# Sixteen small block moves inside SBUF, or two stores to DRAM and eight gathers: the rows of the global tokens

## The chip, the cores and the metric

The program runs on one core of a Trainium2 chip. The metric is the device time of one execution in microseconds (us), lower is better; the time of the kernel before is the median of three runs. A profiled execution comes with a trace, and times inside it are counted from the start of its span.

## The reference

Banded attention with a few global tokens, then two multilayer perceptrons, all in float32:

```python
# attention: 4 batches, 8 heads, 512 local rows (a band of +-32 keys and the 32 global keys),
# 32 global rows that see all 544 keys; head size 64
x = attn_out.transpose(0, 2, 1, 3).reshape(B * S, H * D)      # 2176 rows of 512
h = x @ w_in                                                  # 512 -> 2048
g = np.where(h > 0.0, h, np.exp(np.minimum(h, 0.0)) - 1.0)
x = g @ w_out                                                 # 2048 -> 512
h = x @ w_in2
g = np.where(h >= 1, h, np.where(h <= -1, 0.0, (h + 1) ** 2 / 4.0))
y = g @ w_out2
```

## The kernel before

Precision is kept by splitting each float32 operand into a high and a low part of the type that TensorE multiplies at full rate; a product is three matmuls (low weight by high data, high by low, high by high). The 2176 rows fall into 4 x 512 local rows, handled as wide tiles of 128 x 512, and 4 x 32 = 128 global rows, called group `GR`, handled apart. This change touches only the global rows.

For the local rows one layer is: matmuls up (`up`, lines L283 and L1107; most pairs go through a scheme of seven products instead of eight on pre-added forms of the operands, the tiles `form` in DRAM and `xh`, `xl` in SBUF, loaded at L1070), the activation on ScalarE (L303 to L310) and VectorE (`join`, L315 and L317), a split into `gh` (ScalarE, L332) and `gl` (VectorE, L336), and matmuls down (`dn`, L370). A finished down bank leaves PSUM through ScalarE into `ev` (L349) and from there by DMA into a sum in DRAM: a plain store from the SP queue (L352), or an accumulating DMA from the POOL queue (L354). The last part of a layer is added on VectorE instead (L357, tiles `sum` and `sums`).

The global rows go through the same layers eight times, each time for four blocks of 128 hidden columns; these eight passages are called stages 1 to 8 here. In a stage the operands of the up product stand the other way round (`row_products`, L295): the 128 rows are on the partitions of the result, 4 x 128 hidden columns beside them. The down product (`down_rows`, L383) needs the hidden columns on the partitions, so each 128 x 128 block must be transposed. VectorE transposes 32 x 32 blocks in place (L1201, tile `blocks`), and 16 DMAs from the SP queue put the blocks where they belong (L1207, tile `turned`). Then ScalarE makes the high part and VectorE the low part of `turned`, and TensorE may begin L383.

What sets the order: up to the end of attention instructions stand in the order written. From there (some 200 us into the span until the end) a scheduler places them on each engine's queue by its own estimate of durations; each engine then runs its queue strictly in order, and the SP queue, which issues nearly all DMAs, does too. A DMA from SP also waits for the DMA that stands eight before it on that queue to have landed. Buffers that matter: `u` (6 buffers: `blocks`, `turned` and the partial sums), `gh`/`gl` (6 each), `wraw` (2, packed weights as loaded at L869).

Of the kernel before, what the change touches and what calls it, by code (L numbers as in the profile page):

```python
# [9 lines left out]
F32 = mybir.dt.float32  # L10
BF16 = mybir.dt.bfloat16
F32R = mybir.dt.float32r
U32 = mybir.dt.uint32
U64 = mybir.dt.uint64
AF = mybir.ActivationFunctionType
ALU = mybir.AluOpType
# [5 lines left out]
B, H, SL, SG, D = 4, 8, 512, 32, 64  # L22
# [4 lines left out]
P = 128  # L27
# [51 lines left out]
def band_attention_then_two_mlps(  # L79
# [45 lines left out]
    dram = ctx.enter_context(tc.tile_pool(name="dram", bufs=1, space=bass.MemoryType.DRAM))  # L125
# [29 lines left out]
    eng = pinned  # L155
# [106 lines left out]
    def h_tile(name):  # L262

        i = held[0] // 2 % (H_EARLY + (H_MORE if len(h_p) > 1 else 0))
        held[0] += 1
        return h_p[i >= H_EARLY].tile([P, SL], F32R, tag=name, name=name)
# [159 lines left out]
    def mpool(name, bufs, **kw):  # L426
        return ctx.enter_context(tc.tile_pool(name=name, bufs=bufs, reuse_waits="tile", **kw))
# [4 lines left out]
    with ExitStack() as actx:  # L432
# [371 lines left out]
        for n in range(len(units) + 2):  # L804
# [25 lines left out]
            if n == 1:  # L830
                rows = eye_sb.rearrange("p (c h r) -> p c h r", c=2, h=2)
# [14 lines left out]
        eng = free  # L846
# [4 lines left out]
    u_p = mpool("u", 6, side="right")  # L851
# [332 lines left out]
    def rows(layer, fs, pieces):  # L1184

        def begin():
            need(lambda: all(piece in rows_in for piece in pieces))
            n = len(fs) * P
            u = Up(layer, None, GR, n=n)
            u.row_products(pieces)  # L1190
            u.curve()
            u.join()
            soon.setdefault(now[0] + 1, []).append(lambda: blocks(u))
            item[1] = now[0] + 4
            item[2] = u

        def blocks(u):

            n = len(fs) * P
            t = u_p.tile([P, SL], F32, tag="u", name="blocks")  # L1200
            eng.vector.transpose(t[:, :n], u.g)  # L1201
            u.g = u_p.tile([P, SL], F32, tag="u", name="turned")[:, :n]
            for e in range(4):
                out = u.g[32 * e:32 * e + 32].rearrange("p (f r q) -> p f r q", r=4, q=32)
                for r in range(4):
                    src = t[32 * r:32 * r + 32, :n].rearrange("p (f e q) -> p f e q", e=4, q=32)
                    eng.sync.dma_start(out[:, :, r], src[:, :, e])  # L1207
            u.high()
            u.low()

        item = ["rows", None, None, layer, fs]
        return begin, item
# [51 lines left out]
    def need(done):  # L1264

        tries = 0
        while not done():
            step(line[0])
            tries += 1
            assert tries < 100, "what is needed is not under way"  # L1270
# [53 lines left out]
    for c in range(7):  # L1324
        at = base + 17 * c
# [110 lines left out]
```

## Time and profile before

| what | us |
|---|---|
| median of three runs (lowest to highest) | 825.73 (824.58 to 828.87) |
| the profiled execution's own time | 829.02 |
| its span in the trace | 827.2 |
| TensorE matmul busy in the span | 804.7 |
| VectorE / ScalarE / POOL busy | 678.8 / 544.3 / 86.5 |
| DMA, mean rate over the span | 211 GB/s |

The profiled execution took 3.29 us longer than the median run, and its own time is 1.82 us longer than its span. Busy times of different engines overlap; matmuls are pipelined, so TensorE's row tells when it had work, not how fast the work went.

### The profile page before, as it was taken

The page shows a single profiled execution, that of the slowest core. Times are in us where ns is not written, and L with a number is a line of the kernel's source. Part 1 is how long each engine was busy: PE and PEld are TensorE (multiplying, and loading weights), DVE is VectorE, ACT ScalarE, POOL GpSimd, SP SyncE. Part 2 cuts the span into 40 slices and gives each one's busy share as a digit, 9 for nine tenths or more (in the row PEclk, how much of TensorE's full clock was granted, in tenths as well). Part 3 has the DMA queues.
Part 4 walks back from the last instruction along what each step waited for, and adds up shares of the span by engine and source line. Part 5 has one row for each costly group of instructions (what it writes and reads, how often), then busy time and mean ns, then how long its engine had stood idle before and what let it go on. Part 6 is the DMA issues. An engine that isn't in the chain of part 4 may idle for free.

```text
span 827.2 us, 15959 instructions
## 1 busy us (share of the span) xinstructions
PE 804.7 (97%) x6038; PEld 659.7 (80%) x6038; DVE 678.8 (82%) x1271; ACT 544.3 (66%) x928; POOL 86.5 (10%) x146
## 2 busy tenths in 40 slices
PE   7889899999999999999999999999999999999998
PEld 4667678888887888888888788888888888888876
DVE  4879888997987999966879999999997798745464
ACT  4778875765655667555636687777867786666361
POOL 2222210000011030301100000000110203011000
PEclk9999999999999999999999999999999999999999
DMA  8988845878686498829917948347871996289523
GB/s 268 288 268 252 276 152 186 331 278 311 199 327 103 124 281 279 177 39 225 331 45 254 377 152 314 111 146 260 266 172 33 264 317 108 36 198 289 185 104 115
DMA packets 82109, 174.60 MB, mean 211 GB/s; under 512 B 27376, under 2 KB 27632, under 8 KB 80880
## 3 DMA queue, kind: packets, MB, share of 16 engines
q1 hardware_dynamic: 72528, 156.53, 55.4%
q0 software_dynamic: 9216, 16.78, 13.0%
q8 instruction: 48, 0.79, 0.4%
q10 hardware_dynamic: 288, 0.26, 0.1%
q14 instruction: 29, 0.24, 0.1%
HBM read 112.46 MB, written 58.98 MB: 207 GB/s over the span
## 4 chain that ended last, share of the span: by engine, by line
PE 78%; DMA 8%; ACT 5%; DVE 5%; SPq 3%; issue 2%; ACTq 0%; DVEq 0%
PE dn L370 36%; PE up L1107 25%; PE up L283 4%; PE up L295 2%; SPq L1207 2%; PE dn L383 2%; PE s L147 2%; DMA turned<-blocks 2%; ACT sn L147 1%; DMA wraw<-in_w 1%; PE po L147 1%; DMA form<-xl 1%; PE pt L147 1%; DVE sum L357 1%; PE up L147 1%
## 5 line engine op out<-in xcount | busy, mean ns | idle before, releaser
L370 PE MATMUL dn<-gh,wo 128*128 128x512 f32 x608 | 182.8, 390 | 0.9 <-DVE sums L357 0.9
L863 DVE TENSOR_TENSOR u<-up,u 128x512 f32<-128x512 f32 x182 | 121.7, 683 | 35.7 <-PE up L1107 34.9
L1107 PE MATMUL up<-xh,ws 128*128 128x512 f32 x416 | 140.2, 389 | 0.2 <-DVE u L863 0.2
L370 PEld LDWEIGHTS dn<-gh,wo 128*128 128x128 f32 x608 | 113.8, 188 | 24.7 <-DVE sums L357 1.3
L1107 PE MATMUL up<-xh,wi 128*128 128x512 f32 x376 | 126.1, 389 | 0.0
L354 POOL DMA_DIRECT2D sum<-ev x64 | 58.2, 1188 | 581.8 <-ACT ev L349 553.8
L370 PE MATMUL dn<-gl,wo 128*128 128x512 f32 x304 | 113.4, 389 | 0.0
L332 ACT ACTIVATE gh<-g 128x512 fp32r<-128x512 f32 x123 | 76.7, 628 | 45.6 <-DVE g L315 26.5
L336 DVE TENSOR_TENSOR gl<-g,gh 128x512 fp32r<-128x512 f32 x123 | 83.6, 683 | 11.6 <-ACT gh L332 11.3
L1107 PEld LDWEIGHTS up<-xh,ws 128*128 128x128 f32 x416 | 78.1, 188 | 16.8 <-DVE u L863 0.6
L1107 PEld LDWEIGHTS up<-xh,wi 128*128 128x128 f32 x376 | 70.6, 188 | 14.6
L1107 PE MATMUL up<-xl,ws 128*128 128x512 f32 x208 | 80.9, 389 | 0.0
L1107 PE MATMUL up<-xl,wi 128*128 128x512 f32 x188 | 73.2, 389 | 0.0
L308 ACT ACTIVATE g<-u,half_sb 128x512 f32<-128x512 f32 x56 | 40.4, 722 | 39.9 <-DVE u L863 36.5
L370 PEld LDWEIGHTS dn<-gl,wo 128*128 128x128 f32 x304 | 57.1, 188 | 11.9
L349 ACT ACTIVATE ev<-dn 128x512 f32<-128x512 f32 x96 | 53.0, 598 | 15.1 <-PE dn L370 14.5
L370 PE MATMUL dn<-gh,xl 128*128 128x512 f32 x160 | 62.4, 390 | 0.1
L370 PE MATMUL dn<-gh,xh 128*128 128x512 f32 x160 | 62.3, 389 | 0.0
L370 PE MATMUL dn<-gl,xh 128*128 128x512 f32 x160 | 60.9, 390 | 0.0
L317 DVE TENSOR_TENSOR g<-u,g 128x512 f32<-128x512 f32 x56 | 38.4, 685 | 19.7 <-ACT g L310 19.6
L309 ACT ACTIVATE g<-g,one_sb 128x512 f32<-128x512 f32 x68 | 49.0, 721 | 1.5
L303 ACT ACTIVATE g<-u 128x512 f32<-128x512 f32 x48 | 30.2, 629 | 27.2 <-DVE u L863 23.7
(195 smaller groups left out, 1525.1 us busy)
## 6 DMA issues: line engine op xcount, KB each, us to landing
wraw<-in_w SPq DMA_DIRECT2D x56, 512.0 KB, 7.5
xh<-form SPq DMA_DIRECT2D x42, 512.0 KB, 9.0
xl<-form SPq DMA_DIRECT2D x42, 512.0 KB, 8.0
v_sb<-in_vwin SPq DMA_DIRECT2D x64, 260.0 KB, 4.8
sum<-ev POOLq DMA_DIRECT2D x64, 256.0 KB, 7.9
form<-xh SPq DMA_DIRECT2D x24, 512.0 KB, 4.8
form<-xl SPq DMA_DIRECT2D x24, 512.0 KB, 5.5
sum<-ev SPq DMA_DIRECT2D x32, 256.0 KB, 4.6
```

The source lines that it names most:

```text
L147: return lambda *args, **kw: tc.keep_in_program_order(fn(*args, **kw))
L283: eng.tensor.matmul(self.ps, w, x, start=k == 0, stop=k == 3 * KT - 1)
L308: eng.scalar.activation(self.g, self.ps, AF.Relu, bias=half_sb, scale=-0.5)
L309: eng.scalar.activation(self.g, self.g, AF.Relu, bias=one_sb, scale=-1.0)
L317: eng.vector.tensor_tensor(g, self.ps, g, ALU.max)
L332: eng.scalar.activation(self.gh, self.g, AF.Copy)
L336: eng.vector.tensor_tensor(self.gl, self.g, self.gh.bitcast(F32), ALU.subtract)
L349: eng.scalar.activation(out, ps, AF.Copy)
L354: eng.gpsimd.dma_start(to, out, accum_op=ALU.add)
L370: eng.tensor.matmul(banks[d], w[:, d * P:(d + 1) * P], g, start=first and k == 0, stop=last and k == 2)
L863: return eng.vector.tensor_tensor(out, a, b, op)
L1107: eng.tensor.matmul(ps, w[:, a, at + k * P:at + (k + 1) * P], x[b][:, k * SL:(k + 1) * SL], start=onto is None and k + t == 0, stop=not mo ...
```

## The change

In each of the eight stages the split into high and low parts is made before the blocks are moved, in the order in which VectorE's transpose left them. The high part goes into a second `u` tile (`high`), the low part is left in `blocks`. Each part is stored to DRAM whole (128 x 512, 256 KB, tile `rows`), and four gathers each read it back from DRAM into 32 partitions of `gh` or `gl` at a time, in runs of 32 elements (128 bytes). ScalarE and VectorE no longer touch the moved data; TensorE waits for the gathers themselves.

```diff
             t = u_p.tile([P, SL], F32, tag="u", name="blocks")
-            eng.vector.transpose(t[:, :n], u.g)
-            u.g = u_p.tile([P, SL], F32, tag="u", name="turned")[:, :n]
-            for e in range(4):
-                out = u.g[32 * e:32 * e + 32].rearrange("p (f r q) -> p f r q", r=4, q=32)
-                for r in range(4):
-                    src = t[32 * r:32 * r + 32, :n].rearrange("p (f e q) -> p f e q", e=4, q=32)
-                    eng.sync.dma_start(out[:, :, r], src[:, :, e])
-            u.high()
-            u.low()
+            low = t[:, :n]
+            eng.vector.transpose(low, u.g)
+            high = u_p.tile([P, SL], F32, tag="u", name="high")[:, :n]
+            eng.scalar.activation(high.bitcast(F32R), low, AF.Copy)
+            eng.vector.tensor_tensor(low.bitcast(F32R), low, high, ALU.subtract)
+            u.gh, u.gl = (h_tile(name)[:, :n] for name in ("gh", "gl"))
+            for out, part in ((u.gh, high), (u.gl, low)):
+                kept = dram.tile([P, n], F32, name="rows")
+                eng.sync.dma_start(kept, part)
+                src = kept.rearrange("(r p) (f e q) -> e p f r q", r=4, e=4, q=32)
+                for e in range(4):
+                    at = out[32 * e:32 * e + 32].rearrange("p (f r q) -> p f r q", r=4, q=32)
+                    eng.sync.dma_start(at.bitcast(F32), src[e])
```

The scheduler places the new instructions elsewhere than the old ones, and others around them. On the SP queue, at stage 1 (`sum` are stores of finished banks, `form` the loads of operands for the next local products), a piece of the difference, - is before and + is the change:

```order
-L352 DMA sum_3_110<-ev 128x512
-L1207 DMA turned<-blocks 32x4x32 x14
+L352 DMA sum_3_110<-ev 128x512 x4
+L1209 DMA rows<-high 128x512
+L1070 DMA xl<-form_0_0_115 128x1024
+L1209 DMA rows<-blocks 128x512
 L1070 DMA xh<-form_0_0_115 128x1024
-L1070 DMA xl<-form_0_0_115 128x1024
+L1213 DMA gh<-rows 32x16x32 x4
+L1213 DMA gl<-rows 32x16x32 x4
```

The 16 moves make way for ten DMAs, the stores come behind all four sums, and two loads of forms, which stood behind the moves, now stand between the stores and ahead of the gathers.

On ScalarE at stage 2, before, the high part of the moved rows (`gh<-turned`) stands in the middle of the queue, ahead of two other splits and three evictions of down banks:

```order
L215 ACTIVATE top<-wraw 128x1024
L349 ACTIVATE ev<-dn 128x512
L332 ACTIVATE gh<-turned 128x512
L332 ACTIVATE gh<-g 128x512 x2
L349 ACTIVATE ev<-dn 128x512 x3
L239 ACTIVATE wo<-top 128x1024
```

In the change the high part is made far ahead of that place, beside the split that follows the transpose:

```order
L303 ACTIVATE g<-u 128x512
L1204 ACTIVATE high<-blocks 128x512
L305 ACTIVATE g<-g,one_sb 128x512
L922 ACTIVATE ws<-mixed 128x1024
L332 ACTIVATE gh<-g 128x512
L215 ACTIVATE top<-wraw 128x1024
```

and where it stood, the evictions follow with nothing of the global rows among them:

```order
L239 ACTIVATE wo<-top 128x1024
L332 ACTIVATE gh<-g 128x512
L349 ACTIVATE ev<-dn 128x512
L215 ACTIVATE top<-wraw 128x1024
L349 ACTIVATE ev<-dn 128x512 x2
```

What moved is the instruction that waited for the moves: nothing on ScalarE waits for a DMA of the global rows any more. On VectorE at stage 8 (`sum<-dn` empties the four down banks of local rows), before:

```order
L317 TENSOR_TENSOR g<-u,g 128x512
L336 TENSOR_TENSOR gl<-turned,gh 128x512
L317 TENSOR_TENSOR g<-u,g 128x512
L863 TENSOR_TENSOR u<-up,u 128x512
L336 TENSOR_TENSOR gl<-g,gh 128x512
L357 TENSOR_TENSOR sum<-dn,sum 128x512 x2
```

and with the change:

```order
L317 TENSOR_TENSOR g<-u,g 128x512 x2
L863 TENSOR_TENSOR u<-up,u 128x512
L336 TENSOR_TENSOR gl<-g,gh 128x512
L357 TENSOR_TENSOR sum<-dn,sum 128x512
L336 TENSOR_TENSOR gl<-g,gh 128x512
```

The low part has left this place; it stands right behind the transpose there.

## Rows read from the trace of the kernel before

**Rows 1.** The page: engines' busy time, TensorE's clock by slices, chain that ended last.
```profile
PE 804.7 (97%) x6038; PEld 659.7 (80%) x6038; DVE 678.8 (82%) x1271; ACT 544.3 (66%) x928; POOL 86.5 (10%) x146
...
PEclk9999999999999999999999999999999999999999
...
PE dn L370 36%; PE up L1107 25%; PE up L283 4%; PE up L295 2%; SPq L1207 2%; PE dn L383 2%; PE s L147 2%; DMA turned<-blocks 2%; ACT sn L147 1%; DMA wraw<-in_w 1%; PE po L147 1%; DMA form<-xl 1%; PE pt L147 1%; DVE sum L357 1%; PE up L147 1%
```
**Rows 2.** Stretches of TensorE: from:to, busy us (matmuls), granted clock, DMA share, GB/s.
```profile
240.00:250.00 10.00, 10.00 (x46) 1.00 0.77 209
...
260.00:270.00 10.00, 8.57 (x38) 1.00 0.50 70
...
460.00:470.00 10.00, 9.12 (x41) 1.00 1.03 394
...
790.00:800.00 10.00, 9.18 (x39) 1.00 0.45 157
```
**Rows 3.** The waits of TensorE: line, who released it, us in total, times, longest.
```profile
PE dn L383 <- ACT ev L349: 1.4, 1, 1.4
...
PE dn L370 <- DVE sums L357: 0.9, 1, 0.9
...
PE dn L383 <- DVE sum L357: 0.7, 1, 0.7
```
**Rows 4.** Timeline of stage 2, ScalarE, then TensorE: start, us, what, [idle before <- releaser].
```profile
262.18 0.63 ACT L332 ACTIVATE gh<-turned 128x512 fp32r<-128x512 f32 x1 [5.76 <-DMA turned<-blocks]
...
263.76 1.55 ACT L349 ACTIVATE ev<-dn 128x512 f32<-128x512 f32 x3
...
265.37 0.50 PE L383 MATMUL dn<-xl,gh 128*128 128x512 f32 x1 [1.43 <-ACT ev L349]
```
**Rows 5.** Timeline of stage 8, VectorE, then TensorE.
```profile
789.53 0.69 DVE L336 TENSOR_TENSOR gl<-turned,gh 128x512 fp32r<-128x512 f32 x1 [6.34 <-ACT gh L332]
...
793.74 1.28 DVE L357 TENSOR_TENSOR sum<-dn,sum 128x512 f32<-128x512 f32 x2
...
795.16 0.47 PE L383 MATMUL dn<-xl,gh 128*128 128x512 f32 x1 [0.66 <-DVE sum L357]
```
**Rows 6.** DMAs of three lines: us to issue, and to landing (min/median/max).
```profile
L1207 SPq DMA_DIRECT2D turned<-blocks x128: 585/599/1557, 204.3 to 785.5; - x128
...
DMA to landing us min/median/max: 1.8/2.2/10.8
...
L406 SPq DMA_DIRECT2D outT<-rows_sum x4: 632/638/645, 806.2 to 808.2; - x4
...
DMA to landing us min/median/max: 2.2/2.2/2.2
...
L352 SPq DMA_DIRECT2D sum<-ev x32: 319/328/1128, 151.7 to 574.0; - x32
...
DMA to landing us min/median/max: 2.4/4.6/9.9
```
**Rows 7.** Timeline of the SP queue at stage 1, then two rows of L383.
```profile
206.50 0.54 SPq L352 DMA_DIRECT2D sum<-ev  x1
207.09 9.13 SPq L1207 DMA_DIRECT2D turned<-blocks  x14
216.32 0.53 SPq L1070 DMA_DIRECT2D xh<-form  x1
...
218.72 0.39 PE L383 MATMUL dn<-wl,gh 128*128 128x512 f32 x1
...
223.25 0.39 PE L383 MATMUL dn<-wh,gl 128*128 128x512 f32 x1
```
**Rows 8.** The moves of stages 2 and 7 on the SP queue, and L383 of stage 7.
```profile
244.36 16.19 SPq L1207 DMA_DIRECT2D turned<-blocks  x16
...
683.49 12.00 SPq L1207 DMA_DIRECT2D turned<-blocks  x16
...
706.44 0.62 PE L383 MATMUL dn<-wo,gh 128*128 128x512 f32 x2
```

## The prediction

> **What bounds the kernel now.** I read the page first. TensorE has work for 804.7 of 827.2 us, and its granted clock is full, 9 in all 40 slices [rows 1] and 1.00 in the stretches quoted [rows 2], the level of 2.4 GHz, so the throttle plays no part. What the change can give back is idle time of TensorE, since the number and the size of its matmuls stay the same. The page's chain that ended last seems to offer more: it lists SPq L1207 with 2% and "DMA turned<-blocks" with 2%, together some 33 us. The second view, TensorE by stretches of 10 us, shows how to take that. Between 240 and 250 us, while the moves of stage 2 are under way, TensorE is busy for all 10.00 us [rows 2]. The chain follows a late DMA back through a time in which TensorE had other work. From 130 to 800 us there are 67 stretches, and 64 of them show at least 9.99; the other three miss 1.43, 0.88 and 0.82 us [rows 2], 3.13 us in all. The third view, the waits of TensorE, names them: ScalarE's eviction at L349 held L383 for 1.4 us, VectorE's sums held L370 for 0.9 and L383 for 0.7 [rows 3]. So 3.1 us, 0.4% of the time, is about all that lies there for any change of this part.
>
> The timelines show which of these belong to the global rows. At stage 2 ScalarE sat idle for 5.76 us until the moves had landed, because the high part of `turned` stood next on its queue. The three evictions behind it ran at 263.76, and TensorE, which needed the last bank, began L383 at 265.37 after 1.43 us of idle time [rows 4]. The global rows' data was not what came last; the queue behind it was. At stage 8 it is VectorE: idle for 6.34 us before the low part of `turned`, then the additions that empty the down banks, up to 793.74 + 1.28 = 795.02, and L383 at 795.16 after 0.66 us [rows 5]. The 0.9 us stands between 460 and 470 us, on the tile `sums` at the change of layer, and no L383 lies in that stretch, so I give it no share.
>
> **The change part by part.** *ScalarE and VectorE.* Each stage keeps one activation and one subtraction of the same size, beside the transpose now, with operands that are ready when it ends. Cost: none in busy time. What goes is the wait of these two queues for the DMAs. In front of TensorE that is worth the 1.43 us of stage 2 and the 0.82 us that the stretch at 790 misses, 2.25 together. The waits of the other six stages were hidden, as only these stretches of TensorE have a gap, so nothing comes of them.
>
> *The SP queue.* Sixteen moves of 0.6 us make 9.6 us at the least; stretches of 12.00 us at stage 7 and 16.19 at stage 2 show them with waits between [rows 6, 8]. Two stores now take some 0.33 us each, like L352, 0.66 in all. The first gather must wait until its store has landed: 2.4 us at the least, 4.6 in the median, 9.9 at the most for such a store of 256 KB [rows 6]. No gather of this kind is in the trace. The nearest for its shape is L406, the same 64 KB in the same 128-byte runs, but into DRAM: 0.64 us to issue, 2.2 to land. Eight gathers make 5.1 us of issue. From the first store's issue to the last landing that is 0.33 + 4.6 + 5.1 + 2.2 = 12.2 us in the median, since the second store lands while the first four gathers are issued; 10.0 us with the quickest store, and 0.33 + 9.9 + 5.1 + 10.8 = 26.1 with the slowest store and the slowest landing of a move [rows 6] in place of 2.2. Before it was about as long: 9.6 us of issue, 1.8 to 2.2 of landing and 1.3 for the two splits that followed, 12.7 to 13.1 at best and 19.2 at stage 2 (from 244.36 to 262.18 [rows 4, 8] and the 1.3). What stands behind on SP, loads of weights and forms, is held about as long as before.
>
> *Who waits now.* TensorE's L383 waits for the gathers itself, and behind it stands everything else on TensorE. So each stage needs its room checked. At stage 7 the moves began at 683.49 and L383 ran at 706.44 [rows 8], 22.9 us for a chain of 12.2, or of 16 beside accumulating DMAs as below: hidden. Stages 3 to 6 and 8 have no gap in front of L383 apart from the one explained, and in them the scheduler leaves L383 126 to 133 matmuls behind the last L295, where it stood 126 to 135 behind it. At stage 2 the moves began at 244.36 [rows 8]; the transpose now stands three places later on VectorE, so the store can go at about 246, and L383 stands four places later than before; without the wait it would begin at 265.37 - 1.43 + 0.9, near 264.9. That is 19 us of room, in which the accumulating DMAs from POOL slow everything (that is why the moves took 16.19). A move issued there took up to 10.8 us to land [rows 6]; I take 16 us for the chain, so no wait, with 3 us to spare.
>
> Stage 1 is tightest. In the change the two stores stand behind four sums, the last of them issued at 206.5 [rows 7], so the first goes at about 207. The two loads of forms between the stores and the gathers need buffers that TensorE frees: by their place on its queue (0.227 us a matmul, as the 20 matmuls from 218.72 to 223.25 show [rows 7]) at 206.7 and 208.4, so they hold SP for little. The sums just ahead found the DMAs nearly idle there, so I take 2.6 us for the store, near its least: gathers issued from 209.6 to 214.7, landed at 217 to 218. L383 stands where it began before, at 218.72, and with the low part 0.5 us later; before, the low part was asked for only at 223.25 [rows 7]. So I take no wait, with 1 us to spare; from below it can't gain, as TensorE did not wait there, and above, with the slowest store, the last gather lands at 207 + 0.33 + 9.9 + 5.1 + 2.2 = 224.5, against 219.2: 5.3 us lost.
>
> *The traffic.* Each stage moves 1 MB where 0.25 MB went, 6 MB more on 174.6 MB. The stretches of 10 us show the DMAs anywhere from 0.50 to 1.03 busy [rows 2], so now and then a load comes later; none of TensorE's three waits was for a load [rows 3]. I take nothing for this by itself.
>
> *The new order.* The scheduler lays out TensorE, ScalarE and VectorE anew from stage 1 to stage 3, and in small steps later. Its order of before left 3.13 us of gaps; another one may leave a gap where there was none. Between nothing and the largest single gap, 1.43 us, I take half, 0.7 us.
>
> *The sum* on the profiled execution: 829.02 - 2.25 + 0.7 = 827.5 us. That execution was 3.29 us above the median run, so the same difference, -1.55 us, on the median: 825.73 - 1.55 = **824.2 us**, 0.2% less. A measurement of this kernel can't tell a change of under about 0.5% (4.1 us) from none.
>
> **A rule that speaks against the change.** Before, runs of 128 bytes went from SBUF to SBUF and landed in 1.8 us when nothing else ran [rows 6]; now they are read from DRAM. The Trainium skill (DMA: Bandwidth & Descriptors, section "Why small descriptors are slow (HBM only)") says that small descriptors cost extra where HBM is one end, and that SBUF to SBUF doesn't suffer so. No run so far shows a read of 128 bytes from DRAM; the writes of L406 at 2.2 us speak for a small penalty. By L406 the sum stands as it is; by the rule gathers would land later, which is the third rival.
>
> **The rivals.** *First, the waits only move* (the order of the new layout leaves as much as it gives, or the evictions at stage 2 wait for something else on ScalarE's queue, such as the L215 that now stands among them): 825.7 us. For it: three gaps of about a microsecond in 670 us are what a layout by estimates leaves anyway. Against: the two gaps have one cause each, and it is taken out.
>
> *Second, the chain is right*: the 2% of L1207's issue and the 2% of landings are real, and half of the shares comes back, 16 us, giving 810 us. For it: the page's list. Against: TensorE's busy stretches, which leave no room for over 3.1 us plus the end of the span.
>
> *Third, slower: the gathers are late for L383.* Place: stages 1 and 2, where the room is 1 and 3 us. Price: 5.3 us at stage 1 as above; at stage 2, 246 + 26.1 = 272 against 264.9, 7 us. It decides when a store takes over some 3.6 us to land at stage 1 (2.6 and the 1 us to spare), or store and gathers together take over 19 us at stage 2. Stage 1 alone, at half its price, gives 824.2 + 2.7 = 826.9; both in full, and the 1.4 us of stage 2 not gained, 824.2 + 1.4 + 12.3 = 837.9. For it: at the busiest times stores took 9.9 us and moves 10.8. Against: at 203 to 216 us the queues were light.
>
> **How the numbers follow.** The forecast has 0.60, the first rival 0.20, the second 0.03, the third 0.17, about half of it within 829.9 us (0.5%). The range goes from the lowest run shown less all three gaps, 824.58 - 3.13 = 821.4, down to 821 in round figures, up to 829.5, which takes in the highest run shown (828.87) with no gain and the part of the third rival that costs less than 4 us; left out are the second rival and the dear half of the third, some 0.12 together, and a little of the spread of runs. Faster by over 0.5% needs more than the gaps hold: 0.05, the second rival and chance. Slower by over 0.5%: 0.09. The rest, 0.86, is within 0.5%.
>
> **What would show it.** Right: no wait of ScalarE or VectorE on a DMA of the global rows; full stretches of TensorE at stages 2 and 8; eight stretches on SP of two stores and eight gathers, 9 to 13 us long; gathers landing in some 2 us at quiet times. Wrong: a wait of L383 for "DMA gh<-rows" or "DMA gl<-rows"; gathers that take far over 0.64 us to issue or several us to land with the DMAs idle; new gaps of TensorE elsewhere, at the form loads above all.

## The result, and the profile after

The change is slower: 833.35 us in the median of six runs (830.90 to 834.25) against 824.59 (822.27 to 828.87, six runs), a ratio of 1.0096 with a 95% interval of 1.0070 to 1.0122, about 8 us. The forecast was 824.2, its range 821.0 to 829.5, with 0.09 on slower. The profiled execution of the change took 830.9 us (span 829.1), the least of the six.

In the change L1202 is the transpose, L1204 and L1205 make the high and the low part, L1209 is the stores, L1213 the gathers. First TensorE by stretches, read as in [rows 2]: from:to, length, busy us (matmuls), granted clock, DMA share, GB/s.

```profile
240.00:250.00 10.00, 10.00 (x46) 1.00 1.05 227
260.00:270.00 10.00, 10.00 (x46) 1.00 0.81 199
460.00:470.00 10.00, 7.63 (x34) 1.00 1.03 315
...
610.00:620.00 10.00, 5.88 (x26) 1.00 1.13 207
620.00:630.00 10.00, 9.82 (x36) 0.83 0.10 40
790.00:800.00 10.00, 10.00 (x46) 1.00 0.57 210
```

And the waits of TensorE that answer to [rows 3]:

```profile
PE dn L383 <- DMA gl<-rows: 4.3, 1, 4.3
PE up L1107 <- DVE wi L241: 2.4, 1, 2.4
...
PE dn L370 <- DVE sum L357: 0.4, 1, 0.4
```

The two gaps that the change was to close are closed: the stretches at 260 and 790, which missed 1.43 and 0.82 us, are full. Two others have come. Between 610 and 620 us, in stage 6, TensorE misses 4.12 us, waiting for the low part's gathers, and in the next stretch the granted clock is 0.83, with 36 matmuls where a full stretch has 46. At the change of layer, between 460 and 470 us, it misses 2.37 us where it missed 0.88, and waits for a weight that VectorE unpacks (`wi`, L241).

The second stretch of stage 6 needs a closer look: TensorE's timeline there, then its stretches of 2 us.

```profile
615.26 0.61 PE L383 MATMUL dn<-wo,gh 128*128 128x512 f32 x2
620.18 0.47 PE L383 MATMUL dn<-wo,gl 128*128 128x512 f32 x1 [4.30 <-DMA gl<-rows]
...
621.55 0.63 PE L383 MATMUL dn<-xh,gh 128*128 128x512 f32 x1
621.98 0.63 PE L383 MATMUL dn<-xh,gl 128*128 128x512 f32 x1
```
```profile
620.00:622.00 2.00, 1.82 (x7) 0.80 0.51 201
622.00:624.00 2.00, 2.00 (x6) 0.50 0.00 0
624.00:626.00 2.00, 2.00 (x9) 0.84 0.00 0
626.00:628.00 2.00, 2.00 (x10) 1.00 0.00 0
```

After the idle time the clock was at 0.50, the level of 1.2 GHz, from about 621 to 624 us; matmuls then started 0.43 us apart (621.55 to 621.98) in place of 0.227. The stretch holds 36 matmuls from 620.18 us on, where 43.4 would fit at 0.227 (the 46 of a full stretch count in two that began before it). The 7.4 that are missing cost 1.7 us, as the granted clock of the stretch says too: 10 x (1 - 0.83) = 1.7. So stage 6 lost 4.3 + 1.7 = 6.0 us, the change of layer 2.37 - 0.88 = 1.5, and 2.25 was won: 5.2 us lost in all. The span is only 1.9 us longer than before because its attention part, which the change doesn't touch, was 3.4 us shorter in this execution: the first L295 stands at 185.6 us here and at 189.0 before. 5.2 - 3.4 = 1.8, and the account closes to 0.1 us.

Why the low part was late is read from the SP queue at stage 6, where the transpose ended at 594.7, and from the landings of the two new lines over all stages.

```profile
595.85 0.85 SPq L869 DMA_DIRECT2D wraw<-in_w  x2
596.79 0.42 SPq L1209 DMA_DIRECT2D rows<-high  x1
597.62 0.69 SPq L1209 DMA_DIRECT2D rows<-blocks  x1
606.84 2.61 SPq L1213 DMA_DIRECT2D gh<-rows  x4
609.55 3.27 SPq L1213 DMA_DIRECT2D gl<-rows  x4
```
```profile
L1209 SPq DMA_DIRECT2D rows<-high x8: 319/326/420, 203.1 to 776.1; - x8
L1209 SPq DMA_DIRECT2D rows<-blocks x8: 319/326/745, 204.6 to 776.8; - x8
...
DMA to landing us min/median/max: 2.0/6.1/10.0
```
```profile
L1213 SPq DMA_DIRECT2D gh<-rows x32: 568/628/1616, 206.2 to 784.1; - x32
L1213 SPq DMA_DIRECT2D gl<-rows x32: 563/636/1688, 210.2 to 786.8; - x32
...
DMA to landing us min/median/max: 2.2/2.9/8.8
```

Four accumulating DMAs from POOL and two loads of weights were in flight when the stores went out; the stores took 10 us, and SP stood until 606.84. A second group of four accumulating DMAs began at 608.42, and the gathers of the low part issued among them landed up to 8.8 us later, at 620.04. That is 25.4 us after the transpose, where TensorE began L383 after 20.6 and asked for the low part after 21.2. In the kernel before the sixteen moves of this stage had all landed 13.1 us after the transpose.

### The profile page after: what moved, and what is told of

It reads as the page before. It is cut to its first block, busy times and chain, and to the rows that moved or that the text cites. A ratio compares the mean times of both kernels' runs of the same rounds, so it can differ in the third digit from the quotient of the medians.

```text
span 829.1 us, 15948 instructions
## 1 busy us (share of the span) xinstructions
PE 807.0 (97%) x6038; PEld 661.8 (80%) x6038; DVE 678.7 (82%) x1271; ACT 544.6 (66%) x928; POOL 89.4 (11%) x146
## 5 line engine op out<-in xcount | busy, mean ns | idle before, releaser
L370 PE MATMUL dn<-gh,wo 128*128 128x512 f32 x608 | 183.0, 390 | 0.0
L1107 PE MATMUL up<-xh,ws 128*128 128x512 f32 x416 | 140.3, 389 | 0.0
L370 PEld LDWEIGHTS dn<-gh,wo 128*128 128x128 f32 x608 | 114.1, 188 | 23.5
L1107 PE MATMUL up<-xh,wi 128*128 128x512 f32 x376 | 126.1, 390 | 2.4 <-DVE wi L241 2.4
L354 POOL DMA_DIRECT2D sum<-ev x64 | 60.8, 1225 | 585.5 <-ACT ev L349 555.4
L370 PE MATMUL dn<-gl,wo 128*128 128x512 f32 x304 | 114.0, 390 | 0.0
L1107 PEld LDWEIGHTS up<-xh,ws 128*128 128x128 f32 x416 | 78.1, 188 | 16.2
L336 DVE TENSOR_TENSOR gl<-g,gh 128x512 fp32r<-128x512 f32 x123 | 83.6, 683 | 7.5 <-ACT gh L332 7.4
L1107 PEld LDWEIGHTS up<-xh,wi 128*128 128x128 f32 x376 | 70.6, 188 | 17.4 <-DVE wi L241 2.8
L1107 PE MATMUL up<-xl,ws 128*128 128x512 f32 x208 | 80.9, 389 | 0.0
L1107 PE MATMUL up<-xl,wi 128*128 128x512 f32 x188 | 73.2, 390 | 0.0
L370 PEld LDWEIGHTS dn<-gl,wo 128*128 128x128 f32 x304 | 57.3, 188 | 12.0
L370 PE MATMUL dn<-gh,xl 128*128 128x512 f32 x160 | 62.2, 391 | 0.4 <-DVE sum L357 0.4
L370 PE MATMUL dn<-gh,xh 128*128 128x512 f32 x160 | 62.3, 389 | 0.0
L370 PE MATMUL dn<-gl,xh 128*128 128x512 f32 x160 | 60.2, 389 | 0.0
```

Of the source, the lines that this page charges most:

```text
L336: eng.vector.tensor_tensor(self.gl, self.g, self.gh.bitcast(F32), ALU.subtract)
L354: eng.gpsimd.dma_start(to, out, accum_op=ALU.add)
L370: eng.tensor.matmul(banks[d], w[:, d * P:(d + 1) * P], g, start=first and k == 0, stop=last and k == 2)
L1107: eng.tensor.matmul(ps, w[:, a, at + k * P:at + (k + 1) * P], x[b][:, k * SL:(k + 1) * SL], start=onto is None and k + t == 0, stop=not mo ...
```

## The experiments

Theory A: the trip through DRAM is late in some stage, because its stores and gathers run beside accumulating DMAs. Theory C: the new layout of the engines' instructions loses the time. Further rivals stand where they came up. `before` in a comparison is the kernel before, run on the same chip beside it.

**The change once more.** No edit.

> The change once more, for a second profile, since the profiled execution (830.9 us) was the fastest of its six. In that one TensorE stood still for 4.3 us in front of the low part of the down product of stage 6, until the last gather had landed, and its clock was halved from 621 to 624 us. Theory A (late gathers): stage 6 again, at 831 to 834 us in all, and where the time is longer the wait there is longer, or stage 7, with 3 us of room, joins it. Theory C (the new layout of the queues as a whole, not the gathers): the same time, with gaps of 1 to 3 us scattered over places that have nothing to do with the gathers, the one of 2.4 us at the change of layer the largest.

Measured: 834.37 us (830.52 to 839.63), ratio 1.0095 (1.0056 to 1.0135). TensorE again, in a profiled execution with a span of 833.8 us:

```profile
460.00:470.00 10.00, 6.61 (x26) 0.92 1.04 308
470.00:480.00 10.00, 10.00 (x42) 0.91 0.50 200
610.00:620.00 10.00, 8.86 (x40) 1.00 0.82 124
620.00:630.00 10.00, 6.20 (x17) 0.66 0.59 145
```

The same two places, each dearer. At stage 6 two waits of L383, 2.2 us for the high and 2.7 for the low part, at the change of layer 3.4 us for `wi`, and a lowered clock behind both. So the gaps belong to the kernel and not to one execution, and their size varies. The one at the change of layer, where no L383 waits, is of the kind that theory C has.

**Weights behind the gathers.** The two loads ahead of the stores at stage 6 are packed weights; here each such load made in `words` stands behind the last gather asked for before it.

```diff
+            if gathered:
+                tc.add_manual_dep(ins.ins, gathered[-1].ins.name, IN_ORDER, reason="behind the gathers")
...
-                    eng.sync.dma_start(at.bitcast(F32), src[e])
+                    gathered.append(eng.sync.dma_start(at.bitcast(F32), src[e]))
```

> The change, with every load of packed weights that comes later in the program kept behind the gathers on the SP queue, where the scheduler had put two of them (512 KB each) ahead of the stores at stages 2, 3, 6 and 7. Theory A says that stage 6 is late because its stores land 10 us after issue, behind those loads and beside four accumulating DMAs: stores now land in 5 to 8 us, the last gather before TensorE asks for it, no halved clock, 824 to 827 us. Theory B (two trips one after the other are too long there whatever stands ahead, because of the accumulating DMAs alone): a wait of 2 us or more stays at stage 6, 830 to 834 us. Theory C: 830 to 834 us with gaps elsewhere.

Measured: 840.38 us, ratio 1.0171 (1.0135 to 1.0207), so worse, and above all that was expected. The stores of stage 6 landed 6.5 and 7.1 us after the transpose in place of 12.1 and 12.8, but the last gather still after 19.1, and L383 waited 1.0 us for the low part. Weights now came late all over: VectorE's L218, the first step of unpacking them, waited for them 40.9 us in all (12.8 in the change), L370 waited 2.5 us for VectorE's `gl`, another up product 1.9 for `wi`. The loads ahead of the stores share in the stores' delay; with them behind, more was lost than won.

**The split early, the moves inside SBUF.** Both parts go by the sixteen old moves each, with no DRAM.

```diff
-                kept = dram.tile([P, n], F32, name="rows")
-                eng.sync.dma_start(kept, part)
-                src = kept.rearrange("(r p) (f e q) -> e p f r q", r=4, e=4, q=32)
...
-                    eng.sync.dma_start(at.bitcast(F32), src[e])
+                    for r in range(4):
+                        src = part[32 * r:32 * r + 32].rearrange("p (f e q) -> p f e q", e=4, q=32)
+                        eng.sync.dma_start(at[:, :, r].bitcast(F32), src[:, :, e])
```

> The split in block order as in the change, but no DRAM: each part goes to its operand buffer in 16 moves inside SBUF, 32 in a stage. No transfer waits for another to land. If reading 128-byte runs from DRAM is what is slow (theory D, the rule on small descriptors), this is the better way: 823 to 827 us. By the issue times (32 x 0.6 = 19.2 us and 1.8 to land, 21 us, against 15 us of room at stage 1 and some 20 at stages 2, 6 and 7) it must be late at stage 1 by some 6 us and by 1 to 4 us elsewhere, each wait of over 4 us with a halved clock behind it: 832 to 842 us.

Measured: 841.31 us, ratio 1.0198 (1.0148 to 1.0248). The 32 moves of stage 1 take 21 us of SP (204.78 to 225.65), L383 waits for the parts four times, 8.1 us together. The clock fell behind waits shorter than the 4 us of the expectation: after 2.55 us at stage 1 it was at 0.50 from 230 to 234 us. The trip through DRAM is the cheaper way to carry two parts.

**One trip, split after it.** The unsplit blocks are stored once and gathered by four DMAs into `turned`; the split follows as before. The edit is against the kernel before.

```diff
             eng.vector.transpose(t[:, :n], u.g)
             u.g = u_p.tile([P, SL], F32, tag="u", name="turned")[:, :n]
+            kept = dram.tile([P, n], F32, name="rows")
+            eng.sync.dma_start(kept, t[:, :n])
+            src = kept.rearrange("(r p) (f e q) -> e p f r q", r=4, e=4, q=32)
             for e in range(4):
                 out = u.g[32 * e:32 * e + 32].rearrange("p (f r q) -> p f r q", r=4, q=32)
-                for r in range(4):
-                    src = t[32 * r:32 * r + 32, :n].rearrange("p (f e q) -> p f e q", e=4, q=32)
-                    eng.sync.dma_start(out[:, :, r], src[:, :, e])
+                eng.sync.dma_start(out, src[e])
             u.high()
             u.low()
```

> The split after the move, as in the kernel before, but the blocks make the trip over DRAM: one store of 256 KB and four gathers in place of 16 moves, half of the change's DMA traffic. A chain of 0.3 + 6 (median landing of the change's stores) + 2.5 + 2.9 + 1.3 for the two splits = 13 us, about that of before. Theory A: no wait of TensorE of over 2 us, 823 to 828 us; the waits of ScalarE and VectorE on the transfer stay, and with them up to 2 us of gaps in front of TensorE. Theory B (any store and gather in series is too long beside the accumulating DMAs): TensorE or ScalarE waits over 4 us for the gathers at stages 6 or 7, 829 us or more.

Measured: 827.10 us, ratio 1.0010 (0.9986 to 1.0034): no difference. The last landing lies 7.4 to 14.7 us after the transpose in all stages, and no L383 waits for a DMA. One store and four gathers are in time everywhere, though at stage 6 a gather took 11.6 us to land; two of each are late in one stage. At the change of layer TensorE waits 1.4 us for `wi` here too.

**Stage by stage.** The next kernels use the change's code in the stages named and the old code in the others.

```diff
+            stage.append(u)
+            if len(stage) in (6,):
```

The tuple is (6,) in the first, (1, 2, 3, 4, 5, 7, 8) in the second, (2, 8) in the third, (4,) in the fourth.

> The change's method at stage 6 alone; the other seven stages keep the sixteen moves. Theory A (the stores and gathers of stage 6 land late beside the accumulating DMAs, and L383 waits for the low part): stage 6 loses its 4 to 6 us by itself, with a wait of L383 for gl<-rows of 3 to 5 us between 610 and 625 and a granted clock near 0.5 behind it; the waits of stages 2 and 8 stay as they were before; 829 to 832 us. Theory B (the doubled traffic of all stages together makes each later): stage 6 alone is not late, at most 1 us of wait; 825 to 827. Theory C (the new layout of the engines' instructions loses it): no wait for gl<-rows; within 1.5 us of the kernel before.

> The change's method at every stage but the sixth, which keeps its sixteen moves. Theory A: no gap of TensorE between 605 and 630, the gains of stages 2 and 8 (about 2 us) come through, and only the gap at the change of layer (0.9 before, 2.4 to 3.4 in the change) stands against them: 823.5 to 826.5 us, the kernel before or up to 1 us better. Theories B and C: still slower by 4 to 8 us, with the waits at other places: 829 to 833.

> The change's method at stages 2 and 8 alone, where the kernel before had waits of 1.4 and 0.7 us in front of L383 behind evictions queued after the splits. Theory A: these two waits go, nothing is late: 2 us less than the kernel before, 822 to 824.5. If the new layout alone decides (C), gaps come up elsewhere and the time is within 1 us of before or above it.

> The change's method at stage 4 alone, the stage in front of the change of layer, where L1107 waited for VectorE's copy wi (L241) for 2.4 and 3.4 us in the two profiles of the change and 460 to 470 us held only 7.6 and 6.6 us of matmuls (9.1 before). If stage 4's own transpose and subtraction on VectorE push that copy back, the wait of L1107 comes up here with 2 to 3 us: 827 to 828.5. If it comes from elsewhere (later weights, or the layout laid anew from stage 1), this stretch is as before, with 9.0 to 9.3 us of matmuls, and the time within 1 us of before.

| kernel | median us | ratio (95%) | waits of TensorE over 0.5 us behind the attention part |
|---|---|---|---|
| stage 6 alone | 833.90 | 1.0095 (1.0080 to 1.0110) | gl<-rows 4.6; ev 1.3 (stage 2); sums 0.6 |
| all but 6 | 830.45 | 1.0059 (1.0036 to 1.0082) | wi 3.0 |
| 2 and 8 alone | 828.64 | 1.0019 (0.9992 to 1.0046) | sums 0.5 |
| 4 alone | 831.30 | 1.0047 (1.0020 to 1.0073) | wi 3.4; ev 1.8; u 1.0 |

Stage 6 alone costs as much as the whole change; theory A holds there, and the rival that the traffic of all stages is needed falls. But without stage 6 the kernel is still 5 us slower, so A as stated falls for the rest: all but 6 was expected at 823.5 to 826.5 by A, at 829 to 833 by C. The two losses, 0.95% and 0.59%, add up to more than that of the whole change (0.96%), and why is not shown. The second place is the change of layer, and stage 4 alone brings it up; its profiled execution is the slowest of its ten runs (834.34 us). With stages 2 and 8 alone both old gaps are gone, and the profiled execution (823.04 us) has no wait over 0.51 us; but the twelve runs spread from 821.96 to 832.45, and what the longer ones lost is in no profile. That expectation (822 to 824.5) was missed in the median, and the cause stays open.

What stage 4 does is read from VectorE with stage 4 alone:

```profile
434.89 0.68 DVE L315 SCALAR_TENSOR_TENSOR g<-u,g 128x512 f32<-128x512 f32 x1
442.17 0.70 DVE L218 TENSOR_SCALAR rest<-wraw 128x1024 uint32<-128x1024 uint32 x1 [6.60 <-DMA wraw<-in_w]
...
472.66 1.22 DVE L241 SCALAR_TENSOR_TENSOR wi<-rest,top 128x1024 fp32r<-128x1024 uint32 x1
```

and from the SP queue of the same kernel:

```profile
421.27 0.32 SPq L1213 DMA_DIRECT2D rows<-high  x1
...
427.02 3.56 SPq L1213 DMA_DIRECT2D rows<-blocks  x1
432.52 2.60 SPq L1217 DMA_DIRECT2D gl<-rows  x4
435.22 1.04 SPq L1103 DMA_DIRECT2D wraw<-in_w  x2
```

The loads of the next packed weights (L1103) stand right behind the gathers. VectorE waits 6.60 us for them at L218, works from there almost without a pause (0.56 us idle) up to L241, and TensorE waits for L241. In the change itself the wait at L218 was 3.78 us. In the kernel before VectorE waited 2.94 us for the split there (L336, `turned`), and L218 not at all.

This tells what VectorE waits for, but not yet why TensorE does. Counted from the transpose of stage 4, L241 ends after 53.2 us in the kernel before, 50.8 in the change and 53.3 with stage 4 alone, so `wi` is made as early as before or earlier, and not pushed back, as had been expected. It is TensorE that asks earlier. TensorE and VectorE in the kernel before, then in the change:

```profile
467.40 1.07 PE L370 MATMUL dn<-gl,wo 128*128 128x512 f32 x4
...
472.21 1.21 DVE L241 SCALAR_TENSOR_TENSOR wi<-rest,top 128x1024 fp32r<-128x1024 uint32 x1
...
479.00 0.39 PE L1107 MATMUL up<-xh,wi 128*128 128x512 f32 x1
```
```profile
462.60 1.07 PE L370 MATMUL dn<-gl,wo 128*128 128x512 f32 x4
...
464.77 1.21 DVE L241 SCALAR_TENSOR_TENSOR wi<-rest,top 128x1024 fp32r<-128x1024 uint32 x1
...
466.03 0.50 PE L1107 MATMUL up<-xh,wi 128*128 128x512 f32 x1 [2.37 <-DVE wi L241]
```

Before, TensorE runs 46 matmuls of L370 and then the first up product on this `wi`, 58.8 us after the transpose; in the change it runs 4 of them and asks for `wi` after 48.5 us. The scheduler has moved twelve up products forward by 42 matmuls. Of the kernels here those with this order wait for `wi`, 1.0 to 3.4 us (the change twice, weights behind, one trip, all but 6, 4 alone, and the two below with stage 4 on POOL's queue); those without it don't. In the change the weights don't come later either: the second L1103 landed 19.0 us after the transpose (19.5 in its second profile) against 19.4 before; with stage 4 alone it landed after 21.5. So theory C holds at the change of layer, and when the weights land decides only how long the wait is in the new order. No run moved TensorE's order alone, and what leads the scheduler to it is not shown.

**Three tests of the two places.** The first uses the change's code in stages 1, 2, 3, 5, 7 and 8. The second is stage 4 alone with its ten DMAs on POOL's queue. The third is stage 6 alone, with POOL's sums written in place of added, so that the partial sums of the earlier pairs are left out.

```diff
+            if len(stage) in (1, 2, 3, 5, 7, 8):
```
```diff
-                    eng.sync.dma_start(kept, part)
+                    eng.gpsimd.dma_start(kept, part)
...
-                        eng.sync.dma_start(at.bitcast(F32), src[e])
+                        eng.gpsimd.dma_start(at.bitcast(F32), src[e])
```
```diff
-                eng.gpsimd.dma_start(to, out, accum_op=ALU.add)
+                eng.gpsimd.dma_start(to, out)
```

> The change's method at stages 1, 2, 3, 5, 7 and 8; stages 4 and 6 keep their sixteen moves. Theory A2 (two places make the whole loss: stage 6, where the low part comes late, and stage 4, where the load of the next weights stands on SP behind stores and gathers): both waits are gone, the runs lie with the kernel before or up to 2 us below it, 823 to 827 us, no wait of L383 for gl<-rows and none over 1 us of L1107 for wi. Rival (the loss is spread over the stages, by the traffic or the new layout): still 3 us or more slower, 829 and above.

> The change's method at stage 4 alone, with its two stores and eight gathers on POOL's queue in place of SP's; TensorE, VectorE and ScalarE keep the order of the kernel with stage 4 alone but for a few neighbours. If SP's queue is what costs stage 4 (the two loads L1103 behind the gathers, VectorE's L218 waiting 6.6 us for them), L218 finds its weights 7 to 12 us earlier, the wait of L1107 for wi (3.4 us there) is gone, and the time is 824 to 827 us. If it is the traffic or the order on VectorE, the wait of L1107 stays at 2 to 3 us and the time at 829 to 831.5.

> The change's method at stage 6 alone, and POOL's transfers of the partial sums write their data in place of adding it (the sums of the earlier pairs are left out; same bytes written, same order on every engine as with stage 6 alone). If the adding is what holds the stores and gathers up beside them, the stores land in 3 to 5 us in place of 10, the last gather within 20 us of the transpose, the wait of L383 for gl<-rows (4.6 us) is gone and the time is 824 to 827 us. If it is only the number of bytes and packets in flight, stores take 8 us or more and the wait stays at 3 to 5 us: 831 to 834.

All but 4 and 6: 825.13 us, ratio 0.9980 (0.9956 to 1.0004). As theory A2 said, the loss is gone; what is won at stages 2 and 8 can't be told from none. TensorE waits 0.4 us for gl<-rows at stage 1 and nothing at the two places. The traces tell a little more than the medians: from the first L295 to the end of the span, without the attention part, this kernel took 635.6 us, and so did the one with 2 and 8 alone, against 638.2 before (one execution each). That is 2.6 us less, near the 2.25 of the forecast.

Stage 4 on POOL: 827.27 us, ratio 1.0016 (0.9996 to 1.0036), against 1.0047 on SP. TensorE waits 1.0 us for `wi`, against 3.4. The size of the step was expected too large: on SP, L1103 went out 14.6 us after the transpose, here after 11.1, because it then waits for a buffer that TensorE's L1107 frees (8.3 us). VectorE's wait at L218 falls from 6.60 to 2.42 us. The second L1103 landed 17.5 us after the transpose, in place of 21.5. So, in the new order of TensorE, which this kernel has too, earlier weights make most of the wait go. The intervals of the two ratios overlap; it is the waits that tell the kernels apart.

Stage 6 without adding: 823.63 us, ratio 0.9970 (0.9951 to 0.9989). The landings of the gathers with stage 6 alone, first adding, then not:

```profile
L1217 SPq DMA_DIRECT2D gh<-rows x4: 574/628/634, 607.1 to 609.1; - x4
L1217 SPq DMA_DIRECT2D gl<-rows x4: 570/712/1055, 609.8 to 612.0; - x4
...
DMA to landing us min/median/max: 2.4/5.1/9.8
```
```profile
L1217 SPq DMA_DIRECT2D gh<-rows x4: 575/628/634, 603.5 to 605.5; - x4
L1217 SPq DMA_DIRECT2D gl<-rows x4: 570/636/675, 606.2 to 608.2; - x4
...
DMA to landing us min/median/max: 2.3/3.6/4.7
```

and TensorE in the second of them:

```profile
610.00:620.00 10.00, 10.00 (x46) 1.00 0.60 187
620.00:630.00 10.00, 10.00 (x46) 1.00 0.00 0
```

The wait is gone, as the theory said, and the last gather lands 19.5 us after the transpose in place of 26.3. One number missed: the stores still take 7.7 to 7.9 us (9.2 to 9.5 with adding) where 3 to 5 were expected. So the adding decides over the gathers, while the stores are held mostly by what else is in flight, the two loads of weights among it. The time is not that of stage 6 alone: without adding anywhere in the kernel the waits of stage 2 (1.3 us) and for `sums` (0.6) are gone too.

**Both places changed.** Every stage but the sixth, stage 4's DMAs on POOL's queue.

```diff
+            queue = eng.gpsimd if len(stage) == 4 else eng.sync
+            if len(stage) in (1, 2, 3, 4, 5, 7, 8):
```

> The change's method at every stage but the sixth, with the stores and gathers of stage 4 on POOL's queue. Theory A2 (stage 6 and SP's hold on the weights at stage 4 make the loss): the wait of L1107 for wi, 3.0 us with stage 4 on SP, falls to 1 us or less, no clock step near 460 to 480 us, and the time is 823.5 to 826.5 us, as with stages 4 and 6 left out (825.1). Rival (the layout on VectorE at stage 4, not SP's queue): the wait of L1107 stays at 2 to 3 us and the time at 829 to 831.

Measured: 825.98 us (821.63 to 829.56), ratio 0.9993 (0.9964 to 1.0021), against 1.0059 with stage 4 on SP. TensorE at the change of layer, first on SP, then on POOL:

```profile
460.00:470.00 10.00, 6.98 (x29) 0.95 1.04 311
470.00:480.00 10.00, 10.00 (x40) 0.88 0.44 175
```
```profile
460.00:470.00 10.00, 8.50 (x37) 1.00 1.04 306
470.00:480.00 10.00, 10.00 (x46) 1.00 0.21 84
```

The wait for `wi` is 1.5 us in place of 3.0 (1 or less was expected), and the clock no longer falls. The intervals of these two ratios don't overlap, so taking the ten DMAs off SP's queue at stage 4 pays in the new order, though it is the new order that makes the wait. At stage 6 the cause is shown by experiment: late gathers, beside accumulating DMAs. No version that does all the work beats the kernel before by more than a measurement can tell.

## Why the prediction was wrong

**What bounds the kernel: right for the kernel before, and used too far.** TensorE's gaps were the right measure of what could be won, and the sentence that the throttle plays no part held for [rows 1]. It did not hold behind the wait of stage 6: the lowered clock added 1.7 us to the 4.3. No term of the sum and no rival priced a lower clock.

**The gains: right.** The waits of ScalarE and VectorE on the DMAs of the global rows are gone, and with them the 1.43 us of stage 2 and the 0.82 of stage 8. The split's new place on ScalarE and VectorE costs nothing that shows there.

**Who waits now: the step that failed first.** "Stages 3 to 6 and 8 have no gap in front of L383 apart from the one explained" tells that the old moves were in time, not how much room a longer chain has. In stage 6 the room was 20.6 us from the transpose to L383, and 0.6 more to the low part. The estimate taken beside accumulating DMAs, 16 us from the first store's issue, would have fitted; the chain took 23.3 from there, or 25.4 from the transpose, within the 26.1 that the prediction had worked out as its own upper bound. "Before it was about as long" did not hold there either: moves and splits made 13.1 + 1.3 = 14.4 us from the transpose. Stage 6 is one of the places where those DMAs run, and its room was the one to be read off beside the bound. The third rival had the right mechanism, late gathers, and the wrong place: it named stages 1 and 2, where no wait of over 0.5 us came; that its prices (826.9 to 837.9 us) take in the measured time is luck. Stage 2 had room, with the last gather 14.6 us after its transpose and L383 at 17.9. At stage 1 the last gather landed 15.3 us after the transpose, 0.5 us behind the first L383 and just when the low part is asked for; profiles of other kernels show 0.2 to 0.4 us of wait there. The DMAs were less idle than the prediction read them (0.77 busy between 204 and 207 us in the kernel before): its stores, taken at 2.6 us, took 3.1 and 5.6 to land, and the 1 us to spare was about nothing.

**The SP queue: right where it was doubted.** "What stands behind on SP, loads of weights and forms, is held about as long as before": at stage 4 L1103 goes out 12.4 us after the transpose, where it went after 11.6, and lands as early.

**The new order: the second step that failed.** That a new order may leave a gap where there was none was right; its size was not. The largest single gap of the old order, 1.43 us, was taken as the most, and half of it, 0.7 us, as the term; the one gap at the change of layer measured 2.37, 1.5 more than before, in the first profile, and 2.5 more without the clock in the second (3.39 us missed between 460 and 470, less 0.88). "In small steps later" was wrong there too: twelve up products stand 42 matmuls further forward, in front of the copy that they need.

**Durations.** The stores' landing had been bounded well (2.4, 4.6 and 9.9 in [rows 6]; 2.0, 6.1 and 10.0 measured), and so had the gathers' issue (0.64 us; 0.63). Landing at 2.2 us is the least; the median is 2.9 and the most 8.8. The chain was summed with medians, where the place that decides is the one where store and gather are both slow.

**The short runs.** By the 2.2 us that a gather takes at the least, reading runs of 128 bytes from DRAM is as quick as L406's writes of them [rows 6] and at most 0.4 us slower than a move inside SBUF. What made the gathers of stage 6 slow was adding beside them; without it they landed within 4.7 us. What the Trainium skill (DMA: Bandwidth & Descriptors, section "Why small descriptors are slow (HBM only)") says of small descriptors did not decide there. At stage 1, before the first accumulating DMA, gathers took up to 6.3 us, and no run shows what part of that the short runs have.

## What to carry to other kernels

Where no wait shows, a trace tells that the present chain fits, not how much longer it may be: read the distance from producer to consumer at every repetition, and hold the chain's upper bound, taken under the transfers in flight there, against the shortest room. When a scheduler lays the queues anew, look on each engine not only at what became later but at who now asks earlier: here VectorE's copy was made 2.4 us sooner after the transpose than before, and TensorE waited for it because it asked 10.3 us sooner. A store followed by a gather of the same data holds the issuing queue until the store has landed (SP stood from 598.31 to 606.84 at stage 6), so look up what stands behind it.

## What the runs showed of the hardware

An idle time of TensorE of 4.3 us was followed by some 3 us at half its clock, which cost another 1.7 us; behind the 2.37 us at the change of layer the clock stayed at 1.00. The accumulating DMAs from POOL (256 KB each) slowed their neighbours at stage 6: gathers of 64 KB took up to 9.8 us beside four of them and at most 4.7 beside the same four as plain writes, and an issue on POOL at stage 6 took 0.86 to 1.46 us with adding, 0.54 to 0.73 without.
